# Hand-over to the experts: gathers of the late rows in another order, the second expert's first block turned ahead, filler products between

## The chip, the cores and the metric

The kernel runs on one core of one Trainium2 chip. The metric is the device time of one launch in microseconds (us); the numbers below are medians of repeated launches on the same chip. A core has five engines that run side by side and meet through semaphores: PE (matrix products, with PEld for loading the stationary operand), ACT, DVE and POOL (elementwise work; POOL also issues gathers and scatters), and SP, which only issues DMAs. Each engine takes its instructions strictly in its own order.

## What is computed

Attention with four sink columns and a window of 128, a gated MLP, and then a layer of eight experts. Only the last is touched:

```python
def _moe2_ref(x, w_skip, w_gate, w1, w2):
    do_compute = x @ w_skip > 0
    xc = x[do_compute]
    logits = xc @ w_gate
    e_idx = argmax(logits, axis=1)
    gate_w = softmax(logits)[range(len(xc)), e_idx]
    for e in range(8):
        mask = e_idx == e
        h = maximum(xc[mask] @ w1[e], 0)        # 512 -> 1024
        y[mask] = gate_w[mask] * (h @ w2[e])    # 1024 -> 512
    out[do_compute] = xc + y
```

There are 1536 tokens (rows) of 512 numbers. Everything is float32; a product in that precision is made of three passes over halves `hi` and `lo` of its operands (hi·hi, hi·lo, lo·hi).

## The kernel before

The MLP's output rows are scattered to a DRAM buffer `xs`, sorted by expert, as they become known (`choose`, L645, an indirect DMA on POOL). The last two tiles of tokens are scattered at the very end of the MLP. For each expert, `load_x(e, b)` (L756) reads rows back: block 0 has 128 rows, block 1 the next 64, and they land in a tile `xg` of a pool of eight. Expert 0's block 0 was read early and is completed in PSUM by `start_x`, so its second read, issued with the late ones, only serves the final addition.

`experts` (L900 on) then runs, for each expert: `block_h` (24 products of 512 columns, L851, into two PSUM banks that DVE empties as `h`, L855), `few_h` (16 products, L814) only where the expert has more than 128 rows, `turn_x` (four transposes on PE, L799, then a `hi` copy on ACT and a `lo` subtraction on DVE, named `xh`/`xl` for block 0 and `xf` for block 1), `block_turn` (eight transposes `htp`, L865, then `hT` on ACT and DVE), `block_y` (24 products, L877), and `few_turn`/`few_y` under the same condition. The condition is a register that each engine reads from the count `cnt` (L920: an instruction TENSOR_LOAD and two more); a skipped body is a COMPARE_AND_BRANCH (L925 for `few_h`, L943 for `few_turn`, L937 for `few_y`), after which PE signals its semaphores once its queue has run dry. Expert 0 has no more than 128 rows, expert 1 has more.

The weights of the experts stream in beside this: `prep2` issues DMAs on SP (L740, 256 KB each, into eleven `stage` tiles), ACT copies each tile to its `hi` half (L68) and DVE or POOL subtracts to get `lo` (L71).

The order of the instructions on each engine isn't the order of the code. A scheduler gives it: it walks a model of the engines and takes, on each, the ready instruction of the highest priority, which falls with the place in the code. So lines moved in `experts` can move anything behind them. `filler` (L428) issues idle products at a priority lowered by 1000, `warm(n)` (L417) issues n idle products of 256 columns at the normal one; both write a PSUM tile that nobody reads. The lines the change touches:

```python
for e in range(2):
    for b in range(2):
        load_x(late, e, b)
...
    if e == 0:
        turn_x(0, 1)
...
    turn_x(e + 1, 0)
    turn_x(e + 1, 1)
```

Of the kernel before, what the change touches and what calls it, by code (L numbers as in the profile page):

```python
# [18 lines left out]
def build(ctx: ExitStack, tc: tile.TileContext, q, k, v, n_sink, window,  # L19
# [47 lines left out]
    def act_copy(out, in_, scale=1.0):  # L67
        nc.scalar.activation(out=out, in_=in_, func=ACTF.Copy, scale=scale)  # L68

    def lo_of(out, in_, hi, eng=None):  # L70
        (eng or nc.vector).tensor_tensor(out=out, in0=in_, in1=hi.bitcast(F32), op=ALU.subtract)  # L71
# [340 lines left out]
    def warm(n, pool=acqp, tag="acq"):  # L412

        if n:
            t = pool.tile([P, 512], F32, tag=tag, name="warm")
            for _ in range(n):
                nc.tensor.matmul(out=t[:, 0:256], lhsT=idle[:, 0:P], rhs=idle[:, 0:256], start=True, stop=True)  # L417
# [313 lines left out]
    def prep2(late, e, piece, gate=()):  # L731

        if piece < 2:
            s = w1[e, :, piece * 512:(piece + 1) * 512].rearrange("(a p) f -> p a f", p=P)
        else:
            s = w2[e, (piece - 2) * 512:(piece - 1) * 512, :].rearrange("(a p) f -> p a f", p=P)
        hi, lo = new_w2(), new_w2()
        for a in range(4):
            st = late.tile([P, 512], F32, tag="stage", name="stage", bufs=11)
            nc.sync.dma_start(out=st, in_=s[:, a])  # L740
            with ExitStack() as es:
                for g in gate:
                    es.enter_context(tc.issue_after(g))
                act_copy(hi[:, a], st)
                lo_of(lo[:, a], st, hi[:, a], nc.vector if a else nc.gpsimd)
        w2t[e, piece] = (hi, lo)
# [3 lines left out]
    def load_x(late, e, b):  # L750

        n = HP if b else P
        t = late.tile([P, RW], F32, tag="xg", name="xg", bufs=8)[0:n]
        r = e * ES + b * P

        (nc.gpsimd if e > 1 else nc.sync).dma_start(out=t, in_=xs[r:r + n, :])  # L756
        xg[e, b] = t
        return t
# [29 lines left out]
    def new_xgt():  # L788
        return [mo.tile([P, KD, P], F32R, tag=f"h{a}", name=f"x{a}") for a in "hl"]

    def sides(t):

        return t[:, :, 0:HP], t[:, :, HP:P]

    def turn_x(e, b):
        n = HP if b else P
        tp = attp.tile([P, KD, P], F32, tag="att", name="xgt")[:, :, 0:n]
        for kk in range(KD):
            nc.tensor.transpose(out=tp[:, kk], in_=xg[e, b][:, kk * P:(kk + 1) * P], identity=ident[0:n, 0:n])  # L799
        if b:  # L800
            xgT[e, b] = late_[0].tile([P, KD, P], F32R, tag="xf", name="xf", bufs=1)
            hi, lo = sides(xgT[e, b])
        else:
            xgT[e, b] = hi, lo = new_xgt()
        act_copy(hi, tp)
        lo_of(lo, tp, hi)


    def few_h(e):
        for half in range(2):  # L810
            ps = acqp.tile([P, 512], F32, tag="acq", name="hps")
            for kk in range(KD):
                for m, w_ in enumerate(w2t[e, half]):
                    nc.tensor.matmul(out=ps, lhsT=xgT[e, 1][:, kk, :], rhs=w_[:, kk, :], start=kk == 0 and m == 0, stop=kk == KD - 1 and m == 1)  # L814
            act_copy(h2[e, 1][half], ps)

    def few_turn(e):
        hi, lo = sides(hT[e, 1])
        for half, h in enumerate(h2[e, 1]):
            tp = attp.tile([P, 4, P], F32, tag="att", name="htp")  # L820
            for c in range(4):
                nc.tensor.transpose(out=tp[:, c], in_=h[:, c * P:(c + 1) * P], identity=ident)
            r = slice(4 * half, 4 * half + 4)
            s = late_[0].tile([P, 4, HP], F32, tag="hs", name="hs", bufs=2)
            act_copy(s, tp[:, :, HP:P])
            nc.vector.tensor_tensor(out=s, in0=tp[:, :, 0:HP], in1=s, op=ALU.add)
            nc.scalar.activation(out=hi[:, r], in_=s, func=ACTF.Relu)
            nc.vector.scalar_tensor_tensor(out=lo[:, r], in0=s, scalar=0.0, in1=hi[:, r].bitcast(F32), op0=ALU.max, op1=ALU.subtract)

    def few_y(e):  # L830
        y = gvp.tile([P, 512], F32, tag="gv", name="yps")
        for c in range(NF2):
            for m, w_ in enumerate(w2t[e, 2 + c // 4]):
                nc.tensor.matmul(out=y, lhsT=hT[e, 1][:, c, :], rhs=w_[:, c % 4, :], start=c == 0 and m == 0, stop=c == NF2 - 1 and m == 1, skip_group_check=True)

        t = late_[0].tile([P, 512], F32R, tag="ys", name="ys", bufs=1)
        act_copy(t, y)
        nc.tensor.matmul(out=y[0:HP], lhsT=upper[HP:P], rhs=t[HP:P], start=False, stop=True, skip_group_check=True)
        o = new_row(mo)[0:HP]
        add_row(o, xg[e, 1], y[0:HP])  # L840
        put_row(o, xg[e, 1], put_out)

    def block_h(e):

        xh, xl = xgT[e, 0]
        ps = [accp.tile([P, 512], F32, tag="acc", name="hps") for _ in range(2)]
        for half in range(2):
            wh, wl = w2t[e, half]
            for kk in range(KD):
                for m, (x_, w_) in enumerate(((xh, wh), (xh, wl), (xl, wh))):  # L850
                    nc.tensor.matmul(out=ps[half], lhsT=x_[:, kk, :], rhs=w_[:, kk, :],  # L851
                                     start=kk == 0 and m == 0, stop=kk == KD - 1 and m == 2)

        for half in range(2):
            nc.vector.tensor_scalar(out=h2[e, 0][half], in0=ps[half], scalar1=0.0, scalar2=None, op0=ALU.max)  # L855

    def block_turn(e):
        for half, h in enumerate(h2[e, 0]):
            turn_h(hT[e, 0], h, half)
# [10 lines left out]
    def block_y(e):  # L870

        hh, hl = hT[e, 0]
        y = gvp.tile([P, 512], F32, tag="gv", name="yps")
        for c in range(NF2):
            wh, wl = w2t[e, 2 + c // 4]
            for m, (h_, w_) in enumerate(((hh, wh), (hh, wl), (hl, wh))):
                nc.tensor.matmul(out=y, lhsT=h_[:, c, :], rhs=w_[:, c % 4, :], start=c == 0 and m == 0, stop=c == NF2 - 1 and m == 2)  # L877
        o = new_row(mo)
        add_row(o, xg[e, 0], y)
        put_row(o, xg[e, 0], put_out)  # L880
# [20 lines left out]
    def experts(late):  # L901

        late_[0] = late
        rv = {}
        for e in range(2):
            for b in range(2):
                load_x(late, e, b)
        for piece in range(2):
            prep2(late, 0, piece)
        for e in range(NE + 1):  # L910
            if e < NE:
                for b in range(2):
                    h2[e, b] = [(late if b else mo).tile([P, 512], F32, tag="hm" if b else "th", name="h2", bufs=2) for _ in range(2)]
                t = xtp.tile([P, 2, NF2, P], F32R, tag="xt00", name="hT")
                hT[e, 0] = t[:, 0], t[:, 1]
                hT[e, 1] = xtp.tile([P, NF2, P], F32R, tag="xt10", name="hT")
                block_h(e)
                if e == 0:
                    turn_x(0, 1)
                rv[e] = nc.values_load(cnt[0:1, e:e + 1], engines=ENG, min_val=0, max_val=NT)  # L920
            if e + 1 < NE:
                for piece in range(2):
                    prep2(late, e + 1, piece, anchors if e == 0 else ())
            if e < NE:
                with tc.If(rv[e] > P):  # L925
                    few_h(e)
            if e + 1 < NE:
                turn_x(e + 1, 0)
                turn_x(e + 1, 1)
            if e > 0:  # L930
                block_y(e - 1)
            if e < NE:
                block_turn(e)
                for piece in range(2, 4):
                    prep2(late, e, piece)
            if e > 0:
                with tc.If(rv[e - 1] > P):  # L937
                    few_y(e - 1)
            if e + 2 < NE:
                for b in range(2):  # L940
                    load_x(late, e + 2, b)
            if e < NE:
                with tc.If(rv[e] > P):  # L943
                    few_turn(e)
# [195 lines left out]
    late = None  # L1140
    for i, (g, t0, t1, c0, c1, want) in enumerate(PHASES):
# [21 lines left out]
        if done == NB_ALL and late is None:  # L1163
            early.close()
            late = fast.enter_context(tc.tile_pool(name="late", bufs=2))
# [4 lines left out]
    count_tokens(attp)  # L1170
    judge()
    experts(late)
    fast.close()
    general()
# [31 lines left out]
```

## Time and profile before

| | us |
|---|---|
| median of 3 runs | 635.26 |
| lowest, highest | 633.27, 635.63 |
| the profiled execution, device time | 634.08 |
| its span, first to last instruction | 632.3 |
| PE busy in the span | 590.3 (93%) |
| DVE busy | 451.4 (71%) |
| ACT busy | 370.8 (59%) |
| POOL busy | 191.0 (30%) |

The profiled execution's time is its span and 1.8 us around it. Times of the trace count from the first instruction. The MLP ends near 465 us, the hand-over to the experts runs from there to about 486 us, and the last product of the last expert ends at 622.9 us. [...] PE idle behind a bracket `[0.83 <-DMA xg<-xs]` means that PE stood for 0.83 us and the gather ended the wait.

### The profile page before, as it was taken

What the parts mean: (1) busy time and instruction counts of PE and PEld (TensorE: products, weight loads), DVE (VectorE), ACT (ScalarE), POOL (GpSimd) and SP (SyncE); (2) the same over time, 40 slices, a digit from 0 to 9 for tenths busy, and PEclk for the clock granted to TensorE, in tenths of its full rate; (3) what the DMA queues carried; (4) which work ended last, traced back from release to release, by engine and by line L of the source; (5) the groups of instructions that cost most, each with busy time, mean ns of one, the idle gap of its engine ahead of it and who ended that gap; (6) DMA issues with size and microseconds to landing.
All of it is one profiled execution on the core that took longest, in us unless ns stands there. A gap on an engine that the chain in (4) does not pass through costs nothing. (4 is left out here: it accounts for less than half of the span.)

```text
span 632.3 us, 10773 instructions
## 1 busy us (share of the span) xinstructions
PE 590.3 (93%) x3449; PEld 474.3 (75%) x3449; DVE 451.4 (71%) x1149; ACT 370.8 (59%) x872; POOL 191.0 (30%) x279
## 2 busy tenths in 40 slices
PE   5889898899999999999999999999997999999993
PEld 3666676668777877777778999899985777777762
DVE  4999889895555585665654577688747697879961
ACT  5788787786545454544553456657615674856730
POOL 4443254465433041101111030021005343537411
PEclk9889998999999999999999999999998999999997
DMA  8668976653010220100004200022108786978901
GB/s 208 147 186 228 259 215 181 200 168 67 0 35 2 84 51 17 36 5 14 1 0 155 96 30 1 1 87 92 33 35 243 250 259 199 338 223 267 345 2 37
DMA packets 78420, 75.81 MB, mean 120 GB/s; under 512 B 43138, under 2 KB 55426, under 8 KB 78352
## 3 DMA queue, kind: packets, MB, share of 16 engines
q1 hardware_dynamic: 75552, 69.32, 36.5%
q0 software_dynamic: 2512, 5.68, 2.7%
q8 instruction: 31, 0.51, 0.3%
q14 instruction: 37, 0.30, 0.2%
q10 hardware_dynamic: 288, 0.00, 0.0%
HBM read 65.37 MB, written 11.98 MB: 122 GB/s over the span
## 5 line engine op out<-in xcount | busy, mean ns | idle before, releaser
L462 PE MATMUL gv<-xt,ring 128*128 128x512 f32 (+1 forms) x1152 | 226.2, 345 | 1.6 <-ACT xt L68 0.8
L462 PEld LDWEIGHTS gv<-xt,ring 128*128 128x128 f32 x1152 | 176.0, 189 | 27.7 <-ACT xt L68 1.1
L68 ACT ACTIVATE ring<-w 128x512 fp32r<-128x512 f32 x144 | 90.3, 629 | 98.0 <-PE gv L462 70.4
L71 DVE TENSOR_TENSOR ring<-w,ring 128x512 fp32r<-128x512 f32 x108 | 74.6, 692 | 41.6 <-ACT ring L68 41.1
L71 DVE TENSOR_TENSOR w<-stage,w 128x512 fp32r<-128x512 f32 x96 | 87.4, 942 | 9.6 <-ACT w L68 7.5
L474 PE MATMUL acc<-ring,hh 128*128 128x512 f32 x288 | 92.5, 402 | 0.0
L68 ACT ACTIVATE w<-stage 128x512 fp32r<-128x512 f32 x128 | 72.9, 626 | 11.9 <-DMA stage<-in_moe_w_dram 8.7
L71 POOL TENSOR_TENSOR ring<-w,ring 128x512 fp32r<-128x512 f32 x36 | 48.5, 1349 | 54.2 <-ACT ring L68 54.1
L321 POOL TENSOR_SCALAR_AFFINE_SELECT pt<-pt 128x256 f32<-128x256 f32 x40 | 19.8, 495 | 138.1 <-ACT pt L68 138.1
L71 POOL TENSOR_TENSOR w<-stage,w 128x512 fp32r<-128x512 f32 x32 | 46.6, 1459 | 48.6 <-ACT w L68 27.0
L474 PEld LDWEIGHTS acc<-ring,hh 128*128 128x128 f32 x288 | 50.8, 188 | 10.8 <-ACT hh L68 0.6
L474 PE MATMUL acc<-ring,hl 128*128 128x512 f32 x144 | 57.2, 399 | 0.0
L290 ACT ACTIVATE p<-p,st 128x132 f32<-128x132 f32 x96 | 38.3, 400 | 31.1 <-DVE st L286 30.4
L877 PE MATMUL yps<-w,hT 128*128 128x512 f32 x192 | 47.1, 399 | 1.0 <-DVE w L71 0.6
L851 PE MATMUL hps<-w,xh 128*128 128x512 f32 x128 | 43.3, 418 | 0.7 <-issue 0.4
L877 PEld LDWEIGHTS yps<-w,hT 128*128 128x128 f32 x192 | 35.3, 188 | 10.4 <-ACTq L925 1.0
L497 DVE TENSOR_TENSOR th<-th,gv 128x512 f32<-128x512 f32 (+1 forms) x48 | 26.5, 552 | 20.7 <-PE gv L462 18.7
L645 POOL DMA_INDIRECT xs<-x,pi x12 | 13.2, 1103 | 81.2 <-ACT ring L68 48.6
L68 ACT ACTIVATE hh<-th 128x512 fp32r<-128x512 f32 (+1 forms) x48 | 25.1, 523 | 16.2 <-DVE th L497 15.7
L496 DVE SCALAR_TENSOR_TENSOR th<-th,gv 128x512 f32<-128x512 f32 (+1 forms) x48 | 26.3, 548 | 8.6 <-ACT th L493 8.6
L474 PEld LDWEIGHTS acc<-ring,hl 128*128 128x128 f32 x144 | 27.0, 188 | 7.0 <-DVE hl L501 0.4
L140 DVE SCALAR_TENSOR_TENSOR w<-w,st 128x512 int32<-128x512 int32 x36 | 30.8, 856 | 1.4
(171 smaller groups left out, 972.2 us busy)
## 6 DMA issues: line engine op xcount, KB each, us to landing
stage<-in_moe_w_dram SPq DMA_DIRECT2D x128, 256.0 KB, 4.5
st<-in_moe_w_gate_dram SPq DMA_DIRECT2D x12, 512.0 KB, 5.6
st<-in_moe_w_val_dram SPq DMA_DIRECT2D x12, 512.0 KB, 4.1
st<-in_moe_w_out_dram SPq DMA_DIRECT2D x12, 512.0 KB, 5.5
xs<-trash SPq DMA_DIRECT2D x8, 387.0 KB
qk<-in_k_dram SPq DMA_DIRECT2D x12, 256.0 KB, 3.9
qk<-in_q_dram SPq DMA_DIRECT2D x12, 256.0 KB, 3.7
vb<-in_v_dram SPq DMA_DIRECT2D x12, 256.0 KB, 3.7
```

Source lines behind the costliest of these rows:

```text
L68: nc.scalar.activation(out=out, in_=in_, func=ACTF.Copy, scale=scale)
L71: (eng or nc.vector).tensor_tensor(out=out, in0=in_, in1=hi.bitcast(F32), op=ALU.subtract)
L140: nc.vector.scalar_tensor_tensor(out=di, in0=di, scalar=3, in1=low, op0=ALU.logical_shift_left, op1=ALU.bitwise_or)
L290: nc.scalar.activation(out=p[:, h], in_=p[:, h], func=ACTF.Exp, scale=-1.0, bias=st[:, h:h + 1], accum_out=st[:, 2 + h:3 + h])
L321: nc.gpsimd.affine_select(out=d[:, 0], in_=d[:, 1], compare_op=ALU.is_ge, fill=0.0, base=0, pattern=[[0, 2], [1, P]], channel_multiplier=-1)
L462: nc.tensor.matmul(out=ps, lhsT=w_[:, kk * P:(kk + 1) * P], rhs=x_[:, kk, t0 * P:t1 * P], start=kk == 0 and m == 0, stop=kk == KD - 1 and ...
L474: nc.tensor.matmul(out=acc[g, t], lhsT=h_[:, s], rhs=w_, start=c == 0 and m == 0, stop=c == NFC - 1 and m == 2)
L496: nc.vector.scalar_tensor_tensor(out=th, in0=th, scalar=1.0, in1=gp, op0=ALU.add, op1=ALU.mult)
L497: nc.vector.tensor_tensor(out=th, in0=th, in1=vp, op=ALU.mult)
L645: d = nc.gpsimd.indirect_dma_start(out=xs[:, :], out_offset=bass.IndirectOffsetOnAxis(ap=pi[:, t], axis=0), in_=x2s[t], in_offset=None, bo ...
L851: nc.tensor.matmul(out=ps[half], lhsT=x_[:, kk, :], rhs=w_[:, kk, :], start=kk == 0 and m == 0, stop=kk == KD - 1 and m == 2)
L877: nc.tensor.matmul(out=y, lhsT=h_[:, c, :], rhs=w_[:, c % 4, :], start=c == 0 and m == 0, stop=c == NF2 - 1 and m == 2)
```

## The change

The four gathers issued on SP after the last scatter go in the order (expert 1, block 0), (0, 1), (1, 1), (0, 0) instead of (0, 0), (0, 1), (1, 0), (1, 1). Expert 1's block 0 is turned right behind expert 0's `block_h`, ahead of expert 0's block 1, and no longer later in the loop. Ten idle products are put before that turn and four behind it.

```diff
-        for e in range(2):
-            for b in range(2):
-                load_x(late, e, b)
+        for e, b in ((1, 0), (0, 1), (1, 1), (0, 0)):
+            load_x(late, e, b)
...
                 block_h(e)
                 if e == 0:
+
+                    warm(10)
+                    turn_x(1, 0)
+                    warm(4)
                     turn_x(0, 1)
...
             if e + 1 < NE:
-                turn_x(e + 1, 0)
+                if e > 0:
+                    turn_x(e + 1, 0)
                 turn_x(e + 1, 1)
```

The scheduler moves far more than these lines. Three places are shown. The first is PE right behind expert 0's `block_h`; `xg_5378` is block (0, 1) in both kernels, `xg_5380` is (1, 0) before and (1, 1) after, `xg_5376` is (1, 0) after. Before:

```order
L851 MATMUL hps_5427<-w2_5402,xl_5343 128x512
L799 MATMUL xgt_5454<-ident_108,xg_5378 128x64 x4
L920 TENSOR_LOAD cnt_134
L920 ISA x2
L799 MATMUL xgt_5532<-ident_108,xg_5380 128x128 x4
```

After (the line left out stands for the rest of the four idle products):

```order
L417 MATMUL warm_5454<-ident_108 128x256
L799 MATMUL xgt_5465<-ident_108,xg_5376 128x128 x4
L417 LDWEIGHTS ident_108
L417 MATMUL warm_5474<-ident_108 128x256
...
L799 MATMUL xgt_5479<-ident_108,xg_5378 128x64 x4
L923 TENSOR_LOAD cnt_134
L923 ISA x2
L851 MATMUL hps_5646<-w2_5500,xh_5470 128x512
L851 MATMUL hps_5646<-w2_5501,xh_5470 128x512
L851 MATMUL hps_5647<-w2_5518,xh_5470 128x512
L799 MATMUL xgt_5557<-ident_108,xg_5380 128x64 x4
L851 MATMUL hps_5646<-w2_5500,xl_5471 128x512
```

Expert 1's block 0 is now turned first and three of expert 1's products (`hps_5646`, `hps_5647`) stand ahead of the turn of its block 1. Of the ten `warm` products only one stands here; the other nine were moved ahead of `block_h`, where seven of the ten `filler` products had stood.

The second place is DVE at the same time (`w_5475`/`w_5476` and `w_5493`/`w_5494` are the `hi`/`lo` halves of expert 1's first weights before, `w_5500`/`w_5501` and `w_5518`/`w_5519` after; `h_5420` and `h_5421` empty expert 0's two banks). Before:

```order
L71 TENSOR_TENSOR w_5476<-stage,w_5475 128x512 x3
L855 TENSOR_SCALAR h_5420<-hps 128x512
L71 TENSOR_TENSOR w_5494<-stage,w_5493 128x512 x3
L855 TENSOR_SCALAR h_5421<-hps 128x512
L71 TENSOR_TENSOR xf<-xgt,xf 128x4x64
L71 TENSOR_TENSOR w_5564<-stage,w_5563 128x512
L920 TENSOR_LOAD cnt
L925 COMPARE_AND_BRANCH
L925 UNCONDITIONAL_BRANCH x2
L71 TENSOR_TENSOR xl<-xgt,xh 128x512
```

After:

```order
L71 TENSOR_TENSOR w_5501<-stage,w_5500 128x512 x2
L855 TENSOR_SCALAR h_5420<-hps 128x512
L71 TENSOR_TENSOR w_5501<-stage,w_5500 128x512
L71 TENSOR_TENSOR w_5519<-stage,w_5518 128x512 x2
L855 TENSOR_SCALAR h_5421<-hps 128x512
L71 TENSOR_TENSOR w_5519<-stage,w_5518 128x512
L71 TENSOR_TENSOR xl<-xgt,xh 128x512
L71 TENSOR_TENSOR xf<-xgt,xf 128x4x64
```

`xl` of expert 1 now comes ahead of `xf` of expert 0 and one weight tile earlier; the six weight subtractions and two `h` ahead of it are the same.

The third place is PE behind expert 0's `block_y`. Before (`htp_5775` and `htp_5782` are expert 1's `block_turn`, `hps_5882` is expert 2's `block_h`; the body left out is skipped):

```order
L877 MATMUL yps_5745<-w2_5581,hT_5424 128x512
L865 MATMUL htp_5775<-ident_108,h2_5624 128x128 x3
L937 COMPARE_AND_BRANCH
...
L937 UNCONDITIONAL_BRANCH x2
L865 MATMUL htp_5775<-ident_108,h2_5624 128x128
L865 MATMUL htp_5782<-ident_108,h2_5625 128x128 x4
L851 MATMUL hps_5882<-w2_5671,xh_5733 128x512
```

After (three reads of `cnt` and seven idle products stand where one of each is shown, two reads between the first skipped body and L947; the bodies left out are skipped down to the last branch, behind which expert 1's `few_h` runs):

```order
L877 MATMUL yps_5761<-w2_5597,hT_5424 128x512
L923 TENSOR_LOAD cnt_134
...
L428 MATMUL warm_5290<-ident_108 128x256
L928 COMPARE_AND_BRANCH
...
L923 TENSOR_LOAD cnt_134
...
L947 COMPARE_AND_BRANCH
...
L941 COMPARE_AND_BRANCH
...
L928 COMPARE_AND_BRANCH
L814 MATMUL hps_5724<-w2_5500,xf_5562 128x512
```

The skips of expert 0's `few_h`, `few_turn` and `few_y`, five of PE's eight reads of `cnt` and seven of the low-priority idle products now stand in a row between expert 0's `block_y` and expert 1's `few_h`. Before, expert 1's `few_h` stood in the middle of its `block_h`, and the turn of expert 2 was followed by expert 0's `block_y`; after, the turn of expert 2 follows expert 1's `few_h` and is followed at once by expert 2's `block_h`, which needs it.

## Rows read from the trace of the kernel before

**Rows 1.** PE in time (start, us, engine, line, what, idle before), 480 to 488 us.
```profile
480.88 0.46 PE L799 MATMUL xgt<-ident,xg 64*128 64x64 f32 x4 [0.83 <-DMA xg<-xs]
482.15 0.66 PE L799 MATMUL xgt<-ident,xg 128*128 128x128 f32 x4 [0.81 <-DMA xg<-xs]
485.28 0.66 PE L799 MATMUL xgt<-ident,xg 64*128 64x64 f32 x4 [2.48 <-DMA xg<-xs]
485.86 2.07 PE L851 MATMUL hps<-w,xh 128*128 128x512 f32 x4
```

**Rows 2.** By stretch: its length, busy PE, PEld, DVE, ACT, POOL, granted clock, DMA, GB/s.
```profile
480.04:485.28 5.24, 1.12 (x10) 0.77 (x9) 5.24 (x8) 1.52 (x4) 2.48 (x4) 0.97 1.00 243
485.28:491.70 6.42, 6.42 (x22) 5.22 (x23) 3.32 (x7) 3.88 (x8) 1.58 (x1) 0.50 1.05 348
...
102.70:106.10 3.40, 1.92 (x9) 1.25 (x8) 3.40 (x7) 1.50 (x3) 0.79 (x1) 1.00 0.18 49
106.10:109.50 3.40, 3.40 (x17) 2.81 (x18) 2.41 (x9) 2.25 (x7) 0.17 (x1) 0.50 0.91 262
119.80:123.10 3.30, 1.80 (x11) 1.52 (x11) 2.38 (x11) 1.69 (x7) 0.81 (x3) 1.00 0.87 305
123.10:126.50 3.40, 3.40 (x20) 2.55 (x18) 2.50 (x6) 3.40 (x7) 2.21 (x4) 1.00 0.16 57
```

**Rows 3.** SP and POOL in time: the four late gathers, then POOL's.
```profile
477.26 2.13 SPq L756 DMA_DIRECT2D xg<-xs  x4
...
479.02 1.18 POOL L756 DMA_DIRECT2D xg<-xs  x2
```

**Rows 4.** DVE in time, the last steps before expert 1's products.
```profile
483.18 0.68 DVE L855 TENSOR_SCALAR h<-hps 128x512 f32<-128x512 f32 x1
483.78 0.41 DVE L71 TENSOR_TENSOR xf<-xgt,xf 128x256 fp32r<-128x256 f32 x1
...
484.71 0.68 DVE L71 TENSOR_TENSOR xl<-xgt,xh 128x512 fp32r<-128x512 f32 x1
```

**Rows 5.** PE's sequencer reads `cnt` and skips a body, 481.7 to 483.5 us (start: last two).
```profile
L920 PEldq TENSOR_LOAD <-cnt x1: 309/309/309, 482.1 to 482.1; - x1
...
L925 PEldq COMPARE_BRANCH  x1: 362/362/362, 482.8 to 482.8; - x1
L925 PEldq EVENT_SEMAPHORE  x1: 51/51/51, 483.3 to 483.3; - x1
```

**Rows 6.** PE around skipped bodies of later experts, and one read of `cnt`.
```profile
529.70 0.40 PE L851 MATMUL hps<-w,xl 128*128 128x512 f32 x1
530.24 0.70 PE L851 MATMUL hps<-w,xh 128*128 128x512 f32 x2
...
551.90 1.02 PE L799 MATMUL xgt<-ident,xg 128*128 128x128 f32 x8 [0.69 <-DVE w L71]
...
L920 PEldq TENSOR_LOAD <-cnt x1: 343/343/343, 600.0 to 600.0; - x1
...
604.38 5.82 PE L877 MATMUL yps<-w,hT 128*128 128x512 f32 x24 [0.58 <-DVE w L71]
```

**Rows 7.** Idle products on PE in the hand-over.
```profile
471.38 0.82 PE L428 MATMUL warm<-ident 128*128 128x256 bf16 x6
```

**Rows 8.** PE in time, expert 1's `few_h`, expert 2's turn, expert 0's `block_y`.
```profile
493.56 3.97 PE L814 MATMUL hps<-w,xf 128*128 128x512 f32 x16 [0.32 <-PEq L943]
...
499.44 0.99 PE L799 MATMUL xgt<-ident,xg 128*128 128x128 f32 x8
500.36 5.85 PE L877 MATMUL yps<-w,hT 128*128 128x512 f32 x24
```

**Rows 9.** ACT in time, behind expert 1's `few_h`.
```profile
497.62 0.60 ACT L68 ACTIVATE h<-hps 128x512 f32<-128x512 f32 x1 [1.26 <-PE hps L814]
498.12 2.71 ACT L68 ACTIVATE w<-stage 128x512 fp32r<-128x512 f32 x5
500.72 0.59 ACT L68 ACTIVATE xh<-xgt 128x512 fp32r<-128x512 f32 x1
```

## The prediction, made before the changed kernel ran

> **What bounds the kernel now.** I read the page's engine shares first: PE is busy 93% of the span, so time is to be had only where PE stands or runs slowly. [...] PE in time shows what it stands for: three turns of gathered rows, at 480.88, 482.15 and 485.28, behind waits of 0.83, 0.81 and 2.48 us, and then expert 1's first products at 485.86, four in 2.07 us [rows 1]. The wait costs 4.1 us, and the slow stretch costs half of 6.42, 3.2 us. So 7.3 us is all there is to win here.
>
> What ends last in that wait? The gathers are issued on SP from 477.26, four in 2.13 us [rows 3], and the turns of the second and third of them start at 480.88 and 482.15 [rows 1]. But DVE is busy for all 5.24 us of the stretch [rows 2]: it empties the second bank (`h`) only at 483.18 and gets to `xl`, the half that expert 1's fourth kind of product needs, at 484.71 [rows 4]. So two chains end close together: the fourth gather, for which PE waits until 485.28, and DVE's `xl` at 485.39.
>
> **The change, part by part.** I count against the profiled execution, 634.08 us; the median of the runs lies 1.2 us above it.
>
> Gathers. Expert 1's block 0 becomes the first of the four and its block 1 the third. Nothing in the rows lets the first land later than the second did, so it is turned at about 480.8, with `xh` from ACT at about 482. The third landed at 482.15 at the latest. Expert 0's block 0 goes last and is needed only at the end of `block_y`, 15 us later: free.
>
> DVE. Ahead of `xl` stand the same six weight subtractions and two `h`, and `xf` and one weight now stand behind it. So `xl` starts where `xf` did, 483.8, and takes 0.68 [rows 4]: 484.5, and PE goes on at 484.6 instead of 485.28. That is 0.7 us gained, and no more, because DVE is the later chain. Three of expert 1's 24 products need only `xh` and are done before: at full speed 0.23 us each (5.85 us for 24 [rows 8]), 0.7 us gained.
>
> Idle products. Two more than before stand ahead of `start_x`'s products, at 0.82/6 = 0.14 us each [rows 7]; they push ACT's and DVE's weights by at most 0.3 us, which the 0.1 us hand-over margins above hold in part: I take 0.1 us lost. The five around the turns lie in a wait and cost nothing; without that wait they would cost 0.7.
>
> Behind `block_y(0)`. Here the scheduler's new order puts work in a row that had been spread. Seven idle products: 0.8 to 1.0 us. The skip of `few_h(0)`: PE's queue has to run dry, then 0.2 to 0.5 us (482.8 to 483.3 [rows 5]). Then two reads of `cnt`, each 0.7 us from TENSOR_LOAD at 482.1 to the branch at 482.8 [rows 5]: 1.4 us with nothing queued on PE. Then two more skips and the branch of `few_h(1)`, 0.9 us together by the same rows. The three reads ahead of the idle products I take at nothing: PE's queue still holds products then, as at 600.0, where the read was over long before the products queued ahead of it [rows 6]. Sum 0.9 + 0.2 + 1.4 + 0.9 = 3.4 us lost. Bounds: 1.0, where the reads hide too and only idle products and one skip are left; 4.8, where the three first reads show their 0.7 each as far as they exceed the queue. I take 3.4, nearest to the row at 482.1, where PE had nothing queued either.
>
> Beside it, `xf` of expert 1 can only be written when PE has passed `few_h(0)`. DVE needs 0.4 us for its half [rows 4], ACT about the same for the other, which the reads and skips cover; if these hide, 1.2 us of it shows instead.
>
> The branch at 493.56 with its 0.32 us [rows 8], and a skip of 0.15, go from the middle of `block_h(1)`: 0.5 gained.
>
> Expert 2's turn. Before, `block_y(0)` with its 5.85 us lay between the turn at 499.44 and the products that need it [rows 8]. Now they follow at once. From the end of `few_h(1)` ACT has to do the second `h` (0.60), two weights (0.54 each) and `xh` (0.59) [rows 9], 2.4 us with hand-over, while PE has only the turn, 0.99 us [rows 8]: 1.4 us lost. Bounds: 0, if ACT took `xh` first, which its order forbids, and 2.2, if a weight tile is late as well.
>
> Later experts. All eight reads of `cnt` on PE are now made by expert 2; before, skipped `few_h` of later experts had one at the same place and PE stood for 0.69 (551.90, another like it at 571.29) and 0.58 us (604.38), where a skip without a read cost 0.14 (529.70 + 0.40 to 530.24) [rows 6]. Three times about 0.5: 1.5 us gained. PE sets the end there, so it counts in full. DVE and ACT, though, idle in the hole behind `block_y(0)` and convert two or three tiles later; PE waits little for them now, and I add 0.3 us (0 to 1.5).
>
> Sum without the clock: −0.7 −0.7 +0.1 +3.4 −0.5 +1.4 −1.5 +0.3 = +1.8 us.
>
> The clock. The slow stretch cost 3.2 us. Between 480 and 484.6 PE now has 2.5 us of work (the turns' 1.1, five idle products at 0.14, three products at 0.23) instead of 1.1, so the stretch may go. But a new thin place arises behind `block_y(0)`, 3.4 us with 0.9 of idle products in it. The rows show both outcomes at like shares: 1.92 us busy of 3.40 before the clock fell at 106.10, 1.80 of 3.30 where it stayed at 1.00 [rows 2]. The thin place before `few_h(1)` is nearer to the one at 480.04 (1.12 of 5.24), which was followed by 0.50, than to either. So the likeliest is one slow stretch, in the new place. Its price lies between half of 3.40, the one from 106.10, and 3.2, the one at 485.28 [rows 2]: I take 2.2.
>
> Forecast: 634.08 + 1.8 − 3.2 + 2.2 = 634.9 us.
>
> [...]
>
> **The rivals.**
>
> *A, the clock stays at 1.00 throughout.* For it: 2.5 us of work in the first thin place, idle products in the second. Against: the shares above. Price: no 2.2: 632.7.
>
> *B, the hole behind `block_y(0)` is small.* The sequencer gets through the reads while the products and idle products are still queued, and no skip waits long: 1.0 instead of 3.4 us, and with so little thin work the clock stays: 632.7 − 2.4 = 630.3. For it: the read at 600.0 [rows 6]. Against: two of the reads stand behind a skip, which waits for an empty queue.
>
> *C, slower: the clock falls in both places.* Mechanism: the wait between 480 and 484.6 ends as the one before did, at 0.50, and `block_h(1)` runs slowly as now; then the hole behind `block_y(0)` does it again to `few_h(1)`. It decides if the granted clock is 0.50 both around 486 and at `few_h(1)`. Price: 632.7 + 3.2 + 2.2 = 638.1, and 639.1 with the long stretch twice.
>
> *D, the gather put first lands late.* Four gathers, POOL's two at 479.02 [rows 3] and the weights come within 3 us, and the DMA share is 1.00 over the stretch [rows 2]; the last one was waited for until 485.28. If the first lands that late, then the turn (0.66), `xh` (0.6) and `xl` (0.68) follow one another, PE goes on at about 487.5 instead of 484.6, and the time is 637.8. Against: arrivals came in the order of issue. [...]
>
> **How the numbers follow.** Forecast 634.9, chance 0.46, its own range 633 to 637. A 0.19 (632.7). B 0.14 (630.3). C 0.16 (638.1). D 0.05 (637.8). The range 630.6 to 638.5 leaves out the lower part of B and the upper part of C, about 0.2 together, and holds the bounds 1.0 to 4.8 of the hole in all other cases. A measurement of this kernel can tell about 0.5% from no change, here 3.2 us around 635.26: below 632.1 is faster, above 638.4 slower. Faster: all of B and a third of A, 0.20. Slower: less than half of C, a third of D and 0.05 for the rest of the unknown, 0.14. The same: 0.66.
>
> **What would show it.** PE goes on with `xl` products near 484.6 and DVE's `xl` ends just before; if PE goes on earlier, DVE wasn't the later chain. The hole between the last `block_y(0)` product and `few_h(1)`'s first should be 3 to 4 us, with the sequencer's reads in its middle. PE should stand 1 to 2 us ahead of expert 2's first product, for ACT's `xh`. The skips near 551, 571 and 604 should shrink to 0.15. The granted clock near 486 and at `few_h(1)` decides between the forecast, A and C. The forecast is wrong if one of these holes isn't there, or if a later expert's products wait for weights.

## The result and the profile after

The changed kernel takes **643.74 us** (median of 4 runs, 639.98 to 646.62) against 634.26 us (4 runs) of the kernel before: 1.0132, 95% interval 1.009 to 1.0175. That is slower by more than the 0.5% that can be told apart here, and above the predicted range, which ended at 638.5. Beside other experiments, later and on another chip, the same kernel took 647.14 against 633.32 us (1.0223, 1.0191 to 1.0255), so the size of the loss varies and its sign does not.

The profiled execution of the changed kernel takes 643.28 us, 9.2 us more than that of before (634.08). I line the two up by `block_y`, between whose starts both do the same work:

| stretch | before | after | difference | forecast |
|---|---|---|---|---|
| start to `block_y(1)` | 515.26 | 517.44 | +2.2 | +2.0 |
| `block_y(1)` to `block_y(2)` | 22.47 | 26.92 | +4.5 | +0.3 (here and in the next) |
| `block_y(2)` to `block_y(3)` | 15.12 | 18.14 | +3.0 | −0.5 |
| `block_y(3)` to the last product's end | 70.02 | 69.62 | −0.4 | −1.0 |

Up to `block_y(1)`, which holds nearly all that the prediction argued about, the sum is right within 0.2 us; in part that is luck, as two of its terms were off and nearly cancelled (below). The loss lies behind it, where the prediction had one small term.

Of the run on the other chip there is a profile too. It starts `block_y(1)` at 520.73; 2.3 us of the difference lie ahead of the changed place already (`block_h(0)`'s first products at 476.31 instead of 474.01). The two stretches behind it take 44.7 us together, against 45.1 in the first profile of the changed kernel and 37.6 in the kernel before. The loss there is nearly the same both times, 7.1 and 7.5 us.

PE in time in the changed kernel, the hand-over and the place behind `block_y(0)` (start, us, engine, line, what, idle before and its releaser):

```profile
482.51 0.49 PE L851 MATMUL hps<-w,xh 128*128 128x512 f32 x1 [0.55 <-DVE h L855]
483.71 0.46 PE L799 MATMUL xgt<-ident,xg 64*128 64x64 f32 x4 [0.70 <-DVE xl L71]
484.09 0.51 PE L851 MATMUL hps<-w,xl 128*128 128x512 f32 x1
...
491.52 5.74 PE L877 MATMUL yps<-w,hT 128*128 128x512 f32 x24
...
500.72 5.50 PE L814 MATMUL hps<-w,xf 128*128 128x512 f32 x16 [2.68 <-PEq L941]
...
508.50 1.19 PE L851 MATMUL hps<-w,xh 128*128 128x512 f32 x4 [1.45 <-ACT xh L68]
```

The waits of 0.83, 0.81 and 2.48 us [rows 1] are now 0.55 and 0.70, and DVE's `xl` is what ends the second. Behind `block_y(0)` (its last product ends at 497.26) PE stands or runs idle products for 3.5 us until `few_h` of expert 1 at 500.72, and then 1.45 us for expert 2's `xh`. And PE further on:

```profile
517.44 5.84 PE L877 MATMUL yps<-w,hT 128*128 128x512 f32 x24
526.15 0.48 PE L865 MATMUL htp<-ident,h 128*128 128x128 f32 x1 [2.88 <-DVE xl L71]
526.28 5.41 PE L834 MATMUL yps<-w,hT 128*128 128x512 f32 x16
...
555.33 1.23 PE L822 MATMUL htp<-ident,h 128*128 128x128 f32 x8 [1.44 <-DVE hT L71]
...
577.15 0.47 PE L851 MATMUL hps<-w,xh 128*128 128x512 f32 x1 [0.57 <-PEq L928]
```

Two waits for DVE, 2.88 and 1.44 us, that the kernel before didn't have. In the code, `htp` shares a PSUM pool of two buffers with the turned rows, which DVE reads for the next expert's `xl`; the `htp` at 526.15 starts right behind that `xl` (525.42 + 0.68 = 526.10). By stretch (length, busy PE, PEld, DVE, ACT, POOL, granted clock as the share of full speed that the profile records for PE, DMA, GB/s):

```profile
484.00:488.00 4.00, 4.00 (x16) 3.20 (x15) 2.28 (x4) 2.29 (x4) 1.28 (x1) 0.63 1.04 306
488.00:492.00 4.00, 4.00 (x20) 3.11 (x20) 2.74 (x5) 2.98 (x6) 1.00 (x1) 0.94 1.05 364
500.00:504.00 4.00, 3.28 (x11) 2.64 (x12) 0.69 (x1) 0.60 (x1) 2.31 (x3) 0.77 0.50 142
504.00:508.00 4.00, 3.05 (x15) 2.27 (x13) 0.53 (x1) 1.68 (x4) 0.00 (x0) 0.81 0.36 105
524.00:528.00 4.00, 1.85 (x5) 1.56 (x6) 3.69 (x7) 0.63 (x1) 0.00 (x0) 0.75 1.00 363
528.00:532.00 4.00, 3.69 (x13) 2.55 (x12) 0.00 (x0) 0.27 (x1) 0.00 (x0) 0.82 0.49 181
556.00:560.00 4.00, 3.85 (x12) 2.96 (x13) 3.41 (x6) 2.28 (x6) 1.21 (x1) 0.59 0.96 332
```

The granted clock falls in the hand-over (0.63 and 0.94 in its two stretches, about half the loss of before [rows 2]), at `few_h(1)` (0.77 and 0.81; 5.50 us instead of 3.97 [rows 8], 1.5 lost), behind the wait of 2.88 (0.75 and 0.82; `few_y(1)` takes 5.41 us instead of the 3.98 of before, 1.4 lost), and behind the one of 1.44 (0.59; eight products take 3.5 us from 556.70 on, 1.6 lost).

What do ACT and DVE do meanwhile? DVE in time:

```profile
482.97 0.68 DVE L71 TENSOR_TENSOR xl<-xgt,xh 128x512 fp32r<-128x512 f32 x1
...
493.84 1.28 DVE L71 TENSOR_TENSOR w<-stage,w 128x512 fp32r<-128x512 f32 x2
...
500.22 0.69 DVE L71 TENSOR_TENSOR w<-stage,w 128x512 fp32r<-128x512 f32 x1 [1.22 <-ACTq L941]
507.47 1.29 DVE L71 TENSOR_TENSOR w<-stage,w 128x512 fp32r<-128x512 f32 x2 [6.55 <-ACT w L68]
...
525.42 0.68 DVE L71 TENSOR_TENSOR xl<-xgt,xh 128x512 fp32r<-128x512 f32 x1
```

and ACT:

```profile
498.17 0.38 ACT L68 ACTIVATE xf<-xgt 128x256 fp32r<-128x256 f32 x1 [5.20 <-PEq L928]
498.45 1.14 ACT L68 ACTIVATE w<-stage 128x512 fp32r<-128x512 f32 x2
503.38 0.60 ACT L68 ACTIVATE h<-hps 128x512 f32<-128x512 f32 x1 [3.79 <-PE hps L814]
506.32 0.60 ACT L68 ACTIVATE h<-hps 128x512 f32<-128x512 f32 x1 [2.34 <-PE hps L814]
506.82 1.14 ACT L68 ACTIVATE w<-stage 128x512 fp32r<-128x512 f32 x2
```

Between 495.1 and 507.4 DVE subtracts one weight tile. ACT, which makes the `hi` halves DVE needs, first stands for the skipped `few_h(0)` (5.20 us) and then inside `few_h(1)`, whose banks it has to empty (3.79 and 2.34 us); the next weights stand behind that in its queue and start only at 506.82, behind the second bank's `h` (506.32).

### The profile page after: what moved, and what is told of

It reads as the page before. It is cut to its first block, busy times and chain, and to the rows that moved or that the text cites. A ratio compares the mean times of both kernels' runs of the same rounds, so it can differ in the third digit from the quotient of the medians.

```text
span 641.5 us, 10793 instructions
## 1 busy us (share of the span) xinstructions
PE 595.7 (93%) x3463; PEld 477.8 (74%) x3463; DVE 454.2 (71%) x1149; ACT 371.0 (58%) x872; POOL 188.7 (29%) x279
## 5 line engine op out<-in xcount | busy, mean ns | idle before, releaser
L71 DVE TENSOR_TENSOR w<-stage,w 128x512 fp32r<-128x512 f32 x96 | 90.6, 979 | 13.3 <-ACT w L68 7.9
L321 POOL TENSOR_SCALAR_AFFINE_SELECT pt<-pt 128x256 f32<-128x256 f32 x40 | 19.9, 498 | 137.9 <-ACT pt L68 137.9
L71 POOL TENSOR_TENSOR w<-stage,w 128x512 fp32r<-128x512 f32 x32 | 44.4, 1391 | 49.8 <-ACT w L68 33.9
```

Source lines behind the costliest of these rows:

```text
L321: nc.gpsimd.affine_select(out=d[:, 0], in_=d[:, 1], compare_op=ALU.is_ge, fill=0.0, base=0, pattern=[[0, 2], [1, P]], channel_multiplier=-1)
```

## The experiments

**Theory 1** (mine, after the result). `acqp`, the PSUM pool of `few_h`'s two banks, has two buffers, and the tile of the ten low-priority `filler` products holds one until the last of them is issued. Before, all ten fell into waits of the hand-over. The change's fourteen idle products of ordinary priority fill these waits, seven fillers are left over, and `few_h(0)` can only come behind them: that makes the pile of skips and reads behind `block_y(0)`. (That the shared buffer is the reason is read from the code; no run gave the fillers a tile of another pool.) **Theory 2**: the gathers in another order delay the weights on SP. **Theory 3**: the early turn itself is to blame. Four kernels on one chip tell these apart.

Only the gathers:

```diff
-        for e in range(2):
-            for b in range(2):
-                load_x(late, e, b)
+        for e, b in ((1, 0), (0, 1), (1, 1), (0, 0)):
+            load_x(late, e, b)
```

> Only the new order of the four gathers; no early turn, no idle products. PE's order of work is that of before. Theory 1 (the fourteen idle products leave low-priority filler products over, expert 0's few_h can only come behind them, so reads and skips pile up ahead of expert 1's few_h, and ACT and DVE, queued behind it, fall 5 us back with the weights): nothing of that here, so no loss; at most the 0.7 us of the earlier fourth gather is won: 633.5 to 634.5. Theory 2 (the gathers in another order move the weights' transfers on SP, and the weights come late): most of the loss of 9 us is here, 640 or more.

Measured: 634.46 us, 1.0003 (0.9973 to 1.0032). No loss: theory 2 falls.

The change without its idle products:

```diff
-                    warm(10)
                     turn_x(1, 0)
-                    warm(4)
```

> Gathers in the new order and expert 1's block 0 turned ahead, but none of the fourteen idle products. Theory 1: PE's order keeps expert 0's few_h ahead and block_y(0) late, as before; only the front's gain of 1.4 us, the slow stretch stays: 632.5 to 634. No PE wait of over 1 us behind block_y(1). Theory 3 (the early turn itself puts expert 1's parts in the wrong order): 640 or more, with the waits of 2.88 and 1.44 us of the changed kernel.

Measured: 635.21 us, 1.0003 (0.9979 to 1.0027). No loss, so theory 3 falls; no gain either, which theory 1 had wrong by 1 to 2 us. In its profile the clock is 0.50 from 488 to 492 us, where the kernel with the idle products and three fillers (below) has 1.00.

The idle products alone, in the kernel before:

```diff
                 if e == 0:
+                    warm(14)
                     turn_x(0, 1)
```

> The kernel before with fourteen idle products ahead of the turn of expert 0's block 1, gathers and turns as before. Theory 1: the pile of reads and skips ahead of expert 1's few_h is here, so the hole of 3.6 us, the wait for xh of 1.5 us and the later waits behind block_y(1), 4 us with some us of slow clock: 640 to 646, without the front's gain. Theories 2 and 3: no loss but the idle products, 634 to 636.

Measured: 649.49 us, 1.0172 (1.0096 to 1.0249): the whole loss and more, without the new order of the gathers or the early turn. PE in this kernel has the changed kernel's waits to 0.01 us:

```profile
508.93 5.50 PE L814 MATMUL hps<-w,xf 128*128 128x512 f32 x16 [2.68 <-PEq L938]
516.70 1.20 PE L851 MATMUL hps<-w,xh 128*128 128x512 f32 x4 [1.45 <-ACT xh L68]
...
534.35 0.33 PE L865 MATMUL htp<-ident,h 128*128 128x128 f32 x1 [2.87 <-DVE xl L71]
```

The whole change with fewer fillers:

```diff
-        filler(10)
+        filler(3)
```

> The changed kernel with three instead of ten of the low-priority filler products that the end of the MLP issues; gathers, early turn and the fourteen idle products as changed. Theory 1: none of them is left over, expert 0's few_h stays in front, no hole behind block_y(0), no late weights; what is left is the gain of the front, 3.6 us (products from 483.7 on, a shorter slow stretch), less 0.5: 630 to 632. Theories 2 and 3: as the changed kernel, 640 or more.

Measured: 633.08 us, 0.9965 (0.9939 to 0.9991). In its profile all three fillers run before 471.6 us, none is left over, and the skip of `few_h(0)` stands between the first products of expert 1 again. The loss is gone with seven fillers fewer. Its profile, by stretch, has no fall of the clock in the hand-over:

```profile
484.00:488.00 4.00, 2.68 (x14) 1.76 (x14) 2.15 (x5) 1.66 (x4) 0.62 (x1) 1.00 1.05 330
488.00:492.00 4.00, 3.46 (x16) 2.68 (x17) 2.82 (x5) 2.49 (x6) 0.64 (x1) 1.00 1.05 322
```

Is it the time of the idle products or that any is left over? `filler(5)` leaves two:

> The changed kernel with five low-priority filler products instead of ten, two more than in the kernel with three, and both of these are left over behind block_y(0). Theory 1 (what counts is that any filler is left over, since it holds one of the two PSUM buffers that few_h needs): the pile ahead of expert 1's few_h is back with two idle products in it instead of seven, hole 3.0 us, late waits of 2.9 and 1.4 us, 641 to 645. Rival (the time of the idle products themselves): five idle products at 0.14 us less than the changed kernel, and little else than with three, 633 to 635.

Measured: 641.29 us, 1.0112 (1.0057 to 1.0166). Two idle products, 0.27 us of work, bring the loss back:

```profile
501.02 5.31 PE L814 MATMUL hps<-w,xf 128*128 128x512 f32 x16 [2.63 <-PEq L941]
...
526.25 0.33 PE L865 MATMUL htp<-ident,h 128*128 128x128 f32 x1 [2.88 <-DVE xl L71]
```

So theory 1 holds for what sets the order. Why PE waits 30 and 60 us later is the next question. First, DVE's work is taken away there, in a kernel that leaves out the `lo` halves of expert 3's first weights and serves only to find the cause:

```diff
-                lo_of(lo[:, a], st, hi[:, a], nc.vector if a else nc.gpsimd)
+                if piece > 1 or e != 3:
+                    lo_of(lo[:, a], st, hi[:, a], nc.vector if a else nc.gpsimd)
...
-        w2t[e, piece] = (hi, lo)
+        w2t[e, piece] = (hi, lo if piece > 1 or e != 3 else hi)
```

> The changed kernel, but the lo halves of expert 3's first weights are left out (its products take the hi half in their place), which takes six subtractions of 0.85 us from DVE and two from POOL between block_y(1) and expert 3's turn; all else, the pile ahead of expert 1's few_h too, stays. Theory 1a (PE's waits behind block_y(1) and later come from DVE, 5 us behind with the weights): the wait of 2.88 us at 526 and the slow clock behind it go, and the one of 1.44 us at 555 too: 4.3 to 7 us less than the changed kernel, 636.5 to 639.5. Rival (these waits come from the weights' transfers or from ACT): they stay, 642 to 646.

Measured: 637.74 us, 1.0048 (1.0011 to 1.0085). The hole is as it was, the wait behind `block_y(1)` is gone, the one of 1.44 is 0.21, and the slow stretches there are gone with them:

```profile
502.31 3.93 PE L815 MATMUL hps<-w,xf 128*128 128x512 f32 x16 [2.68 <-PEq L942]
...
523.13 0.71 PE L866 MATMUL htp<-ident,h 128*128 128x128 f32 x5
523.60 3.98 PE L835 MATMUL yps<-w,hT 128*128 128x512 f32 x16
```

DVE, then, not the transfers, made these waits. (In this execution `few_h(1)` kept the full clock, 3.93 us, behind the same hole of 2.68 us.)

The terms for the reads of `cnt` were tried twice. With three fillers, each read is put ahead of the `block_y` before it:

```diff
+            if e + 1 < NE:
+                read(e + 1)
             if e > 0:
                 block_y(e - 1)
```

> The changed kernel with three filler products, and each expert's count read ahead of the block_y before it instead of just ahead of the branch, so that the read runs while PE still has 24 products queued. The prediction's term for the reads (a skip behind a read costs 0.69, without one 0.14 to 0.2): the four waits of 0.58 to 0.69 us ahead of turns and block_y shrink to 0.2, 2 us less than the kernel with three fillers: 630.5 to 632. Rival (what PE stands for is the emptying of its queue ahead of the branch, read or not): 633 as with three fillers.

Measured: 635.69 us, 1.0025 (1.0000 to 1.0051). The four waits at turns and at `block_y` did go, and the time didn't: PE now stands for DVE instead, and at a place where two skips follow one another (at 567.78, with no read there). The order of PE is not quite that of the kernel with three fillers, though, and the clock of this execution is 0.74 and 0.83 in the two stretches from 484 to 492 us, where that kernel had 1.00. By the clock that is 1.7 us, and whether the new place of the reads brought it about is open.

```profile
546.84 1.23 PE L822 MATMUL htp<-ident,h 128*128 128x128 f32 x8 [1.30 <-DVE hT L71]
...
567.78 0.47 PE L851 MATMUL hps<-w,xl 128*128 128x512 f32 x1 [0.68 <-PEq L933]
```

And with ten fillers, all eight reads ahead of expert 0's `block_h`:

> The changed kernel with all eight reads of the counts made ahead of expert 0's block_h. PE's order of work has the same pile ahead of expert 1's few_h, without a read in it and with three idle products left instead of seven. The prediction's term for the two reads behind a skip, 1.4 us: PE's wait ahead of expert 1's few_h shrinks from 2.68 to about 1.3 us. If the skips alone make it: 2.3 us or more. The eight reads in a row, 0.7 us each, may cost the front up to 5 us; the late waits of 2.9 and 1.4 us, which this leaves as they are if they come from ACT and DVE queued behind few_h, stay within 1 us. 639 to 646.

Measured: 647.52 us, 1.0215 (1.0161 to 1.0269). The hole:

```profile
508.67 3.98 PE L814 MATMUL hps<-w,xf 128*128 128x512 f32 x16 [1.45 <-DVEq L942]
...
532.58 0.33 PE L865 MATMUL htp<-ident,h 128*128 128x128 f32 x1 [2.87 <-DVE xl L71]
```

2.68 became 1.45: two reads with nothing queued on PE cost 1.2 us, forecast 1.4. But the wait behind `block_y(1)` stayed at 2.87 with a hole 1.7 us shorter (1.2 of reads, 0.4 of idle products), while the later one, near 559 us, was 0.63 instead of 1.44. (The total is no measure of it: PE stood for 4.36 us ahead of `block_h(0)` in this kernel.) So the hole ahead of `few_h(1)` doesn't make the wait behind `block_y(1)`. That led to **theory 1b**: before, `block_y(0)` stood behind `few_h(1)`, and under its 5.85 us [rows 8] ACT and DVE converted the weights that are queued behind `few_h` on both. The change runs `block_y(0)` ahead of `few_h(1)`, where they stand, and the cover is lost. The test is to give it back, with idle products of about the same length, on one side of `few_h(1)` or on the other. Three kernels on one chip; first the changed one again:

> The changed kernel as it is, beside the next two: 641 to 646.

Measured: 647.14 us (646.04 to 649.38), 1 us above what was expected.

Behind `few_h(1)`:

```diff
                 turn_x(e + 1, 1)
+                if e == 1:
+                    with tc.issue_after(turned[2, 1].ins):
+                        warm(43)
```

> The changed kernel with 43 idle products more, 0.135 us each and so 5.8 us, as long as a block_y, between expert 2's turn and its block_h. Theory 1b (before, block_y(0) stood behind expert 1's few_h, and under its 5.85 us ACT and DVE converted the weights that wait behind few_h on both; the change runs block_y(0) ahead of few_h, where they stand): the idle products give that cover back, the waits of 1.45 (xh), 2.88 and 1.44 us and the slow clock behind the last two go, so 5.8 us of idle work are paid back nearly whole: within 2 us of the changed kernel, PE's waits behind block_y(1) under 0.5 us. Rival (the late waits have another cause): 5 to 6 us more than the changed kernel, waits as they were.

Measured: 645.01 us (644.10 to 647.82). PE from the idle products on:

```profile
509.74 4.87 PE L417 MATMUL warm<-ident 128*128 128x256 bf16 x43
...
519.83 1.23 PE L824 MATMUL htp<-ident,h 128*128 128x128 f32 x8 [2.50 <-DVE hT L71]
...
533.14 0.60 PE L867 MATMUL htp<-ident,h 128*128 128x128 f32 x4
```

Ahead of `few_h(1)`, with `filler(53)`:

> The changed kernel with the same 43 idle products more, as low-priority fillers, so that they stand behind block_y(0) and ahead of expert 1's few_h. Theory 1b: there ACT and DVE stand behind few_h's branch, so this time converts nothing: the waits of 1.45, 2.88 and 1.44 us stay, and the time is 4 to 6 us more than the changed kernel (few_h may keep a clock of 1.00, 1.5 us back). Rival (any 5.8 us would have given ACT and DVE time to catch up): the waits go and the time is that of the kernel with the idle products behind few_h.

Measured: 649.02 us (645.38 to 651.03).

```profile
496.77 5.63 PE L428 MATMUL warm<-ident 128*128 128x256 bf16 x50
505.12 5.50 PE L814 MATMUL hps<-w,xf 128*128 128x512 f32 x16 [2.71 <-PEq L941]
...
512.89 1.19 PE L851 MATMUL hps<-w,xh 128*128 128x512 f32 x4 [1.45 <-ACT xh L68]
...
530.54 0.47 PE L865 MATMUL htp<-ident,h 128*128 128x128 f32 x1 [2.85 <-DVE xl L71]
```

Behind `few_h(1)`, 4.9 us of idle work doesn't lengthen the kernel (2.1 us less than the changed kernel by the medians, with ranges that overlap): the waits for `xh`, behind `block_y(1)` and near 555 us are gone, and from `block_y(1)` to `block_y(3)` it takes 37.1 us, as the kernel before (37.6). One new wait of 2.50 us came ahead of that, against what I expected, because the new order puts six weight tiles ahead of `hT` on DVE (6.54 us from 512.54). Ahead of `few_h(1)`, 43 idle products more leave all three waits as they were (1.45, 2.85, and 1.45 near 560 us), and the same stretch takes 44.8 us. The time rose by only 1.9 us where 4 to 6 were expected; with runs of one kernel 3 to 6 us apart, the waits tell more here than the totals. Theory 1b holds.

Two kernels looked for something better than both. Six idle products ahead of the turn instead of ten (with `filler(3)`):

> The changed kernel with three fillers and six instead of ten idle products ahead of the early turn. If the idle products are what keeps the clock at 1.00 behind the hand-over (with none of them it fell to 0.50 from 488 to 492), then fewer lose part of that: the clock falls again for 2 to 5 us, 633.5 to 635.5. If they only cost their own time, 0.5 us is won: 632 to 633.

Measured: 636.31 us, 1.0047 (1.0025 to 1.007). Slower than the kernel before, but why is open: its profiled execution, at 632.98 us, is the fastest of its ten, with the clock at 1.00 from 476 to 580 us, so the profile doesn't show what the others lost.

Expert 1's last weights ahead of its `few_h` in the code:

```diff
+            if e == 1:
+                for piece in range(2, 4):
+                    prep2(late, e, piece)
             if e < NE:
                 with tc.If(rv[e] > P):
                     few_h(e)
```

> The changed kernel with three fillers, and the last two weight pieces of expert 1 written in the code ahead of its few_h instead of behind its block_turn, so that ACT and DVE convert them earlier. If DVE's lag is what PE still waits for (1.25 us on xf behind block_y(1), 0.7 us at three turns), 1 to 2 us less than with three fillers alone: 631 to 632. If the tiles are not free any earlier, the same 633.

Measured: 636.07 us, 1.0039 (1.0008 to 1.0071). The expectation failed: the 1.25 us went, but the three waits at turns stayed, a new one of 0.77 us for `hT` came, and the clock fell again in the hand-over (0.89 and 0.68 in the two stretches from 484 to 492 us).

Last, a control, three fillers in the kernel before, beside the best kernel again:

> The kernel before with three instead of ten low-priority filler products; no part of the change. A control for the kernel with the whole change and three fillers: if its gain comes from the change, this one stays at before's time, 633.5 to 635.5. If it comes from the seven idle products less, 632 to 633.

Measured: 637.53 us, 1.006 (1.0035 to 1.0086).

> The changed kernel with three filler products once more, beside the control: 632 to 633.5, ratio to before 0.995 to 0.999, and under the control by 1 to 2 us.

Measured: 632.50 us, 0.9992 (0.997 to 1.0014). The control is slower than before, not equal. In its profile, without the seven fillers, the clock is down while `start_x` runs, which costs 1.6 us there:

```profile
472.00:476.00 4.00, 4.00 (x21) 3.90 (x20) 0.96 (x4) 1.08 (x3) 1.98 (x2) 0.61 0.34 131
```

That is not shown to be the whole reason: this execution is the fastest of its ten and at 634.03 us no slower than the profiled one of before (634.08).

So with three fillers the change is worth 5 us (632.5 against 637.5 on one chip), but against the kernel before, with its ten, it is 0.35% ahead once and level once. A gain over both is not shown beyond that.

## Why the prediction was wrong, point by point

**DVE, `xl` and the front: right, with the forecast 0.5 us late.** `xl` products were to start at 484.6, 0.7 us earlier than before; they started at 484.09. DVE got to `xl` at 482.97, 0.8 us before the forecast's 483.8: it began its first weight 0.2 us earlier (475.75, against 475.93 before), and the same six subtractions and two `h` took 7.2 us instead of 7.85. `xl` ended at 483.65, with one turn on PE between it and the products. Three products went ahead, and the gather put first did not land late (its turn runs at 479.79 without a wait), so rival D is out.

**The hole behind `block_y(0)`: right.** 3.4 us forecast, 3.5 measured, with its reads and skips in the middle as the sequencer shows (count, duration min/median/max in ns, first and last start):

```profile
L923 PEldq TENSOR_LOAD <-cnt x3: 300/307/308, 492.9 to 494.3; - x3
...
L923 PEldq TENSOR_LOAD <-cnt x3: 298/299/299, 498.3 to 502.2; - x3
...
L947 PEldq COMPARE_BRANCH  x1: 214/214/214, 499.7 to 499.7; - x1
...
L941 PEldq COMPARE_BRANCH  x1: 202/202/202, 500.1 to 500.1; - x1
```

The first line has the three reads ahead of the idle products. They hid, as assumed, under the products of `block_y(0)`. The skip of `few_h(0)` was compared at 495.0 and signalled at 498.1, just behind the end of the last idle product (497.10 + 0.94 = 498.04). 2.68 us of standing is what the skips and the two later reads make, at 498.3 and 499.0. (The third read of the second line, at 502.2, is behind the branch and runs beside `few_h(1)`.) Rival B is out. What the prediction did not see is why the pile is there at all: it took the order as given and did not ask what held `few_h(0)` back.

**The wait for expert 2's `xh`: right**, 1.4 forecast, 1.45 measured.

**The clock: wrong by 1 us in this execution.** The forecast had no slow stretch in the hand-over and one at `few_h(1)` for 2.2. In the profiled execution rival C came true: both fell. By the granted clock the first cost 1.7 us (4.00 × 0.37 + 4.00 × 0.06, the shares missing to full speed in its two stretches), half of the 3.2 of before (half of 6.42 us, at 0.50 [rows 2]), and the second 1.5. Against the 3.2 that went that is 0.0, where −1.0 was forecast; half of the difference came back in the front, which began 0.5 us before the forecast. Rival A is out. But which of forecast and rival comes true varies: in the second profile of the changed kernel, of these two places, only `few_h(1)` ran slowly (5.51 us), and the hand-over had the full clock:

```profile
484.00:488.00 4.00, 3.17 (x16) 2.21 (x17) 3.49 (x7) 0.00 (x0) 0.62 (x2) 1.00 1.01 285
488.00:492.00 4.00, 1.61 (x9) 0.99 (x8) 1.62 (x3) 2.27 (x4) 1.26 (x1) 1.00 1.05 321
```
```profile
491.82 0.66 PE L865 MATMUL htp<-ident,h 128*128 128x128 f32 x4 [2.39 <-DVE hT L71]
```

It was no faster for it. PE stands 2.39 us for DVE's `hT`, and ACT is idle for the whole of 484 to 488 us. (In the first profile ACT has three weight tiles ahead of its `hT` in this place, and it waited 2.42 us for the transfer of the first and 1.12 us for the next two.) From the turn behind `xl` to `block_y(0)` it took 8.87 us, against 7.81 at the lower clock. Four other kernels with this front (five fillers, less work for DVE, and the two with 43 idle products) ran it at full clock in 7.4 to 8.3 us, with waits of 0.95 to 1.77 us for `hT`. So the slow stretch in the changed hand-over can't be priced by the clock alone: in these five profiles, where it is gone, a wait of 0.95 to 2.39 us for `hT` stands in its place.

**"DVE and ACT convert two or three tiles later; +0.3 us (0 to 1.5)": this is the term that failed.** It measured 7.3 us: 2.88 and 1.44 of waiting, 1.4 and 1.6 of slow clock behind them. In the second profile the same two stretches lost 7.1 us. (In the first they come to 7.5 in all: the skip near 551 gave 0.7 back, and 0.8 is in gaps at branches that I did not trace one by one.) The step was half done. For `xh` the prediction saw that `block_y(0)` had been the cover between `few_h(1)` and expert 2 and that the new order takes it away. It did not carry this on to the weights, which lie in the same two queues behind the same branch. The rows were there. From the end of `few_h(1)` to expert 3's `xl` DVE has fourteen or fifteen weight tiles to convert, 0.9 to 1.0 us each, in both kernels. In the kernel before, that `xl` in time on DVE, and the `htp` of expert 2 on PE, which needs its PSUM bank:

```profile
520.39 0.68 DVE L71 TENSOR_TENSOR xl<-xgt,xh 128x512 fp32r<-128x512 f32 x1
```
```profile
521.13 0.55 PE L865 MATMUL htp<-ident,h 128*128 128x128 f32 x3
```

`xl` ends at 521.07, 23.5 us behind `few_h(1)` (493.56 + 3.97 [rows 8]), and PE follows at once: no time to spare, though no bracket shows a wait. In the changed kernel `xl` ends 19.9 us behind `few_h(1)` (506.22 to 526.10), but PE, without `block_y(0)` in between, is there after 17.1 us (at 523.28). The difference is 2.8 us, the wait 2.88. That the lost cover is the cause, and not the hole ahead of `few_h(1)`, is shown by the pair of kernels with 43 idle products: the 7 us are gone with the cover given back, and stay without it. The prediction priced the idle engines instead of the lost cover, and said that "PE waits little for them now", which was true only under that cover.

**Later skips, −1.5 us: mostly wrong.** From `block_y(3)` on 0.4 us was won. The waits behind a read went, but the new order has two skips in a row instead: one ends at 576.6, the next is compared at 576.8, PE reads nothing there, and it stands for 0.57 us all the same. Other branches cost 0.3 us, and DVE's `hT` 0.64 near 608. In the kernel with the reads moved it was alike: two skips in a row for 0.68 us, and DVE's `hT` for 1.30. DVE is close behind PE, so part of what the reads no longer take goes to waits for DVE.

## What to carry to other kernels

A filler of low priority is not free when it holds a buffer: in this kernel, as its code and its order read, whoever shares the pool waits until the filler's last product is issued, and more idle products of ordinary priority elsewhere can be what leaves it over. When an order moves work from behind a branch to ahead of it, look up on every engine what is queued behind that branch, add up its work until the next meeting with PE, and compare it with PE's work that is left in between; the loss shows there, not at the branch. And price a removed wait by what comes next on the engine that is closest behind, here DVE.

## What the runs showed of the hardware that I had not expected

The same hole went both ways with the clock: behind 2.6 to 2.7 us of standing, `few_h(1)` took 5.3 to 5.5 us in six profiles and 3.93 us in that of the kernel with less work for DVE, where PE had stood for 2.68 us too. Behind the wait of 2.85 to 2.89 us it was the same: `few_y(1)` took 5.36, 5.41 and 6.69 us in three profiles and 3.98 us in three others. The price of such a wait in clock can thus be given only as a span, here 0 to 2.7 us. And the idle products of the hand-over are worth more than their time: seven fewer of them in the kernel before cost 0.6% (637.53 us). The clock was 0.61 in the stretch behind them, where the kernel before had 1.00; that is 1.6 us by the clock, and where the median lost the rest of its 3.9 us is open.
